# Sliding-window attention and a wide feed-forward in one pass: a new order of the first steps, a branch inside the last chunk, and products in rows

## The chip, the cores and the metric

One core of a Trainium2 chip runs the kernel. The metric is the device time of one execution in microseconds (us), as the median over runs. The engines are PE (TensorE, matrix products), ACT (ScalarE), DVE (VectorE), POOL (GpSimd) and SP (SyncE, which here issues the transfers). In the profile, PEld is the weight load of PE, and a "q" behind an engine's name marks its sequencer.

## The reference

Attention with a window of 128 positions and 4 sink keys, and behind it a feed-forward layer with softplus:

```python
# batch 4, 8 heads, 768 positions, head_dim 64; n_sink 4, window 128
scores = scale * np.matmul(q, k.transpose(0, 1, 3, 2))
keep = is_sink | in_window               # 0 <= rel < window, or key < n_sink
a = softmax(np.where(keep, scores, -1e9))
attn = np.matmul(a, v)                   # -> x of 3072 tokens x 512
h = x @ w_in                             # 512 -> 2048, weights arrive as float64
g = np.maximum(h, 0.0) + np.log1p(np.exp(-np.abs(h)))
out = (g @ w_out).astype(np.float32)     # 2048 -> 512
```

`n_sink` and `window` are inputs, so the kernel holds two paths: a fast one for the window and sinks that fit its tiling, and a general one.

## The kernel before, in words

The 3072 tokens are cut into 12 chunks of 256 (three for each batch entry). A chunk passes through 8 attention steps, one for each head, and, one chunk behind, through 8 feed-forward steps `s`, one for each 256 columns of the 2048. Every feed-forward product is made of three: each operand is split into a high part and a remainder, and high*high, remainder*high and high*remainder are added up in PSUM. The methods, with the letters by which the order of the work calls them:

- `scores` S, `softmax` T, `normalise` N, `weights_t` W (with `swap` X and `swapped` x, a transposition by way of DRAM), `values` V, `out` O: the attention of one head. In the first two chunks (`EXACT = 2`) heads go in pairs, in full fp32 (`pair_scores` and so on, L246).
- `up` U: 24 matmuls of 256 columns into `h` (L574). `softplus` F: three ACT instructions on 512 elements (L582 to L584). `gate` P: one on DVE (L590), then `gh`, the high part. `residue` R: `gl`, the remainder. `down` D and E (each one half, 6 matmuls of 512 columns into `acc`, L617), two steps (`lag = 2`) behind U.
- `w`, a, c, d, l: the 32 half weights. Each is brought in by a transfer of 512 KB (w), its top halfwords are copied (a), its float32 is put together on DVE (c, L516), its high part is copied (d) and the remainder is subtracted (l, L67).

Engines' instructions are issued in the order in which the program calls the parts. Until step 17 that order is the string `START`; from there it is a row of letters for every step, `STEADY`. Strings such as `WL`, `WT`, `GH`, `NM` say which engine takes the n-th instruction of a kind (A for ACT, V for DVE, P for POOL; past the end the last letter holds). From step `MIXED = 19` on, the letters M and m take U and D/E together: two matmuls of `up`, one of `down`, and so on.

At the front, `_constants` builds three masks from the two sizes, which come by a small transfer of their own on ACT's queue (L88). Two copies of the first heads' `qk` (328 KB each) are issued on SP. At the end, when all outputs have been issued, every engine loads the flag (L1003, `values_load`) and branches around the general path (L1004). DVE has made the flag from the sizes, the scores' maxima and the weights' extremes some steps before the end.

Of the kernel before, what the change touches and what calls it, by code (L numbers as in the profile page):

```python
# [11 lines left out]
F32 = mybir.dt.float32  # L12
# [26 lines left out]
ORDERED = {mybir.EngineType.PE, mybir.EngineType.SP}  # L39

# [38 lines left out]
def _constants(c):  # L79
# [7 lines left out]
    words = cp.tile([P, 2, 2], I32, name="words")  # L87
    nc.scalar.dma_start(words[:].rearrange("p a b -> p (a b)"), c.a["sizes"].broadcast_to([P, 4]))  # L88
# [8 lines left out]
    rel, key, lt, fold, first, r0, r1 = (scratch(n) for n in (P, NS, P, P, P, NS, NS))  # L97
# [23 lines left out]
    pen0, pen1 = scratch(NS), scratch(NS)  # L121
    nc.gpsimd.tensor_scalar(pen0, r0, c.wd, -BIG, ALU.is_lt, ALU.mult)
    nc.vector.tensor_scalar(m2[:, P:], key, c.ns, -BIG, ALU.is_ge, ALU.mult)
    nc.vector.tensor_scalar(m0[:, :P], first, c.wd, -BIG, ALU.is_ge, ALU.mult)
    nc.gpsimd.tensor_scalar(pen1, r1, c.wd, -BIG, ALU.is_lt, ALU.mult)
    nc.vector.tensor_tensor(m0[:, P:], m2[:, P:], pen0, ALU.min)
    nc.vector.tensor_scalar(m1[:, :P], fold, c.wd, -BIG, ALU.is_ge, ALU.mult)
    nc.vector.tensor_tensor(m1[:, P:], m2[:, P:], pen1, ALU.min)
    nc.scalar.copy(m2[:, :P], m1[:, :P])


class _Attention:
# [103 lines left out]
    def pair_scores(self, h, j):  # L236
# [6 lines left out]
        for e in range(2):  # L243
            rows = slice(e * D, e * D + D)
            q = r[rows, KC + j * P : KC + j * P + P]
            nc.tensor.matmul(s[:, e, :w], q, r[rows, j * KW : j * KW + w], start=True, stop=True)  # L246
# [224 lines left out]
def _weight_dma(c, s, k, half):  # L471
# [7 lines left out]
    r = c.wp.tile([P, 4 * WH if c.w64 else 2 * WH], I16 if c.w64 else F32, tag=tag, name=f"{tag}r")  # L479
# [48 lines left out]
def _weight_high(c, e, eng):  # L528
# [4 lines left out]
    c.w[e] = c.wp.tile([P, 2, n // 2, WC // n], F32R, tag=tag, name=tag)  # L533
# [22 lines left out]
class _Moe:  # L556


    def __init__(self, c, chunk):
        self.c, self.chunk = c, chunk  # L560
        self.acc, self.h, self.t, self.g = None, {}, {}, {}
        self.row = chunk * CT

    def up(self, s):
# [4 lines left out]
        h = c.ps_h.tile([P, 2, CT], F32, tag="h", name=f"h{self.chunk}_{s}")  # L569
        prods = [(e, cc, j) for cc in range(4) for e in ("hh", "lh", "hl") for j in range(2)]  # L570
        for k, (e, cc, j) in enumerate(prods):
# [3 lines left out]
            yield  # L575
# [11 lines left out]
    def gate(self, s):  # L587
# [3 lines left out]
        gh = c.mp.tile([P, 2, CT], F32R, tag="gh", name=f"gh{chunk}_{s}", bufs=c.GB)  # L591
        _copy(nc, _turn(c.GH, chunk * FP + s), gh[:], t[:])
        self.g[s] = [gh]

    def residue(self, s):
        c, nc, chunk = self.c, self.c.nc, self.chunk
        _, t = self.t.pop(s)
        gl = c.mp.tile([P, 2, CT], F32R, tag="gl", name=f"gl{chunk}_{s}", bufs=c.GB)
        _sub(nc, c.E["gl"], gl[:], t[:], self.g[s][0][:])
        self.g[s].append(gl)  # L600

    def down(self, s, *js):
        c, nc = self.c, self.c.nc
        if s == 0 and js[0] == 0:
            self.acc = [c.ps_acc.tile([P, DM], F32, tag=f"acc{t}", name=f"acc{self.chunk}_{t}") for t in range(CH)]
# [6 lines left out]
        last = s == FP - 1 and js[-1] == 1  # L612
        for k, (j, t, x, e) in enumerate(prods):
# [6 lines left out]
            yield  # L620
# [11 lines left out]
def _fast(c):  # L632
# [58 lines left out]
    def products(i, name, k, *args):  # L691
        m, s = divmod(i, H)
        if not 0 <= i < n * H:
            return iter(())
        while any(e[:2] == (s, k) for _, e in todo["l"]):
            stage("l")(i)
        return getattr(moe[m], name)(s, *args)

    def dense(*args):
        return lambda i: list(products(i, *args))  # L700

    def mixed(rest):
        def run(i):
            done, live, rounds = object(), True, 6
            if not rest:
                c.mix = products(i, "up", 0), products(i - lag, "down", 1, 0, 1)
# [373 lines left out]
```

## Time and profile before

| | us |
|---|---|
| median of 3 runs (range) | 687.0 (686.83 to 687.04) |
| the profiled execution, its own time | 686.84 |
| span of the profile, first to last instruction | 685.1 |
| PE busy | 664.3 (97%) |
| PEld busy | 592.2 (86%) |
| DVE busy | 542.1 (79%) |
| ACT busy | 477.9 (70%) |
| POOL busy | 446.8 (65%) |
| chain that ended last: PE's share | 83% (acc L617 36%, h L574 36%) |

The shares are averages over a start of some 105 us, in which weights are prepared, a long even middle, and an end. Matmuls are pipelined, so the distance from one start to the next counts, not the length of one.

### The profile page before, as it was taken

Reading aid. Unit: us, or ns where it says so; the run is one execution under the profiler, and the core shown is the slowest. Engines: PE = TensorE matmul, PEld = TensorE weight load, DVE = VectorE, ACT = ScalarE, POOL = GpSimd, SP = SyncE. Lnnn points to the kernel's source line nnn. Section 1 sums busy time; section 2 is a strip of 40 time slices with the busy share of each in tenths; the row PEclk is TensorE's granted clock in tenths of the full one; section 3 lists DMA queues with packets and bytes.
Section 4 is the critical chain, followed back from the end, with each engine's and each line's share of the span. In section 5 each row is a group of like instructions: output and inputs, shape, how many; then the busy total and the mean of one; then the engine's idle time right before and its main releaser. Section 6 shows DMA issues by size and latency. Waiting matters only on the chain.

```text
span 685.1 us, 14176 instructions
## 1 busy us (share of the span) xinstructions
PE 664.3 (97%) x4319; PEld 592.2 (86%) x4319; DVE 542.1 (79%) x1461; ACT 477.9 (70%) x1213; POOL 446.8 (65%) x817
## 2 busy tenths in 40 slices
PE   5999989999999999999999999999999999999995
PEld 3588878999999999999999999999999999999984
DVE  6899977878888888888889888888878888753332
ACT  6999866768677677767777776777777777753331
POOL 7675479678667776795776775786866776762110
PEclk9999999999999999999999999999999999999998
DMA  8996334344344435344444434433443434310001
GB/s 311 351 404 203 103 89 126 87 116 121 102 121 125 113 90 149 97 107 117 114 117 117 125 91 110 137 107 97 131 118 92 141 93 119 100 51 1 32 1 36
DMA packets 97656, 83.33 MB, mean 122 GB/s; under 512 B 51876, under 2 KB 79140, under 8 KB 97572
## 3 DMA queue, kind: packets, MB, share of 16 engines
q1 hardware_dynamic: 97428, 82.35, 41.7%
q8 instruction: 36, 0.59, 0.4%
q14 instruction: 48, 0.39, 0.2%
q10 hardware_dynamic: 144, 0.00, 0.0%
HBM read 65.53 MB, written 16.78 MB: 120 GB/s over the span
## 4 chain that ended last, share of the span: by engine, by line
PE 83%; POOL 0%; ACT 0%; DVE 0%; POOLq 0%; issue 0%
PE acc L617 36%; PE h L574 36%; PE x L444 5%; PE s L264 3%; PE s L263 3%; PE x L438 1%; PE ts L334 0%; POOL wo L67 0%; DVE mt L590 0%; DVE o L61 0%; ACT mt L583 0%; ACT mt L584 0%; ACT mt L582 0%; POOLq L1003 0%; POOL pt L409 0%; POOL pt L406 0%
## 5 line engine op out<-in xcount | busy, mean ns | idle before, releaser
L574 PE MATMUL h<-xh,wi 128*128 128x256 f32 x1536 | 298.2, 282 | 0.3 <-DVE mt L590 0.3
L574 PEld LDWEIGHTS h<-xh,wi 128*128 128x128 f32 x1536 | 269.1, 189 | 30.1 <-issue 1.1
L617 PE MATMUL acc<-wo,gh 128*128 128x512 f32 x768 | 292.5, 395 | 1.8 <-POOL wo L67 1.2
L574 PE MATMUL h<-xl,wi 128*128 128x256 f32 x768 | 152.9, 281 | 0.0
L574 PEld LDWEIGHTS h<-xl,wi 128*128 128x128 f32 x768 | 140.2, 188 | 14.0
L617 PEld LDWEIGHTS acc<-wo,gh 128*128 128x128 f32 x768 | 143.2, 188 | 5.6 <-POOL wo L67 1.5
L617 PE MATMUL acc<-wo,gl 128*128 128x512 f32 x384 | 145.1, 393 | 1.3 <-DVE gl L67 1.3
L63 POOL TENSOR_SCALAR gh<-mt 128x512 fp32r<-128x512 f32 x88 | 54.8, 623 | 133.5 <-DVE mt L590 104.2
L582 ACT ACTIVATE mt<-h 128x512 f32<-128x512 f32 x96 | 57.6, 600 | 106.7 <-PE h L574 106.0
L590 DVE SCALAR_TENSOR_TENSOR mt<-h,mt 128x512 f32<-128x512 f32 x96 | 65.5, 683 | 35.9 <-ACT mt L584 35.9
L67 POOL TENSOR_TENSOR tl<-u,th 128x256 f32<-128x256 f32 x80 | 64.2, 802 | 45.2 <-issue 32.2
L293 ACT ACTIVATE a<-a,stats 128x136 f32<-128x136 f32 x192 | 76.0, 397 | 7.2 <-DVE stats L292 6.7
L617 PEld LDWEIGHTS acc<-wo,gl 128*128 128x128 f32 x384 | 72.3, 188 | 5.5 <-DVE gl L67 2.2
L67 DVE TENSOR_TENSOR kl<-qk,qkh 128x400 fp32r<-128x400 f32 x80 | 73.3, 916 | 2.5
L67 DVE TENSOR_TENSOR gl<-mt,gh 128x512 fp32r<-128x512 f32 x96 | 71.6, 746 | 4.1 <-POOL gh L63 4.1
L67 DVE TENSOR_TENSOR qkh<-qk,qkh 64x256 fp32r<-64x256 f32 x80 | 44.8, 560 | 27.8 <-ACT qkh L59 21.8
L318 POOL TENSOR_SCALAR a<-a,rc 128x128 f32<-128x128 f32 x156 | 58.1, 385 | 7.5 <-DVE rc L307 7.5
L583 ACT ACTIVATE mt<-mt 128x512 f32<-128x512 f32 x96 | 60.8, 633 | 3.0
L584 ACT ACTIVATE mt<-mt 128x512 f32<-128x512 f32 x96 | 60.7, 633 | 3.1
L59 ACT CAST qkh<-qk 128x656 fp32r<-128x656 f32 x80 | 59.1, 739 | 1.4 <-DMA qk<-qk 1.0
L406 POOL TENSOR_SCALAR_AFFINE_SELECT pt<-th 128x256 fp32r<-128x256 f32 x80 | 50.3, 628 | 0.0
L444 PE MATMUL x<-pt,vv 128*128 128x256 f32 (+1 forms) x216 | 47.6, 323 | 0.0
(191 smaller groups left out, 1098.2 us busy)
## 6 DMA issues: line engine op xcount, KB each, us to landing
qk<-qk SPq DMA_DIRECT2D x160, 164.0 KB, 3.1
rows<-xf SPq DMA_DIRECT2D x320, 32.0 KB, 1.6
u<-rows SPq DMA_DIRECT2D x80, 128.0 KB, 2.7
vr<-v SPq DMA_DIRECT2D x32, 192.0 KB, 2.8
out<-o SPq DMA_DIRECT2D x24, 256.0 KB, 2.3
qk<-qk SPq DMA_DIRECT2D x8, 328.0 KB, 5.7
vr<-v SPq DMA_DIRECT2D x16, 128.0 KB, 2.3
wi00r<-w SPq DMA_DIRECT2D x1, 511.8 KB, 5.8
```

Of the source, the lines that this page charges most:

```text
L59: nc.scalar.copy(out, in_)
L63: nc.gpsimd.tensor_scalar(out, in_, 1.0, 0.0, ALU.mult, ALU.add)
L67: (nc.vector if eng == "V" else nc.gpsimd).tensor_tensor(out, a, b, ALU.subtract)
L293: nc.scalar.activation(a, a, AF.Exp, bias=nm, scale=-1.0, accum_out=total)
L318: (nc.vector if eng == "V" else nc.gpsimd).tensor_scalar(a, a, rc[:, j : j + 1], 0.0, ALU.mult, ALU.add)
L444: nc.tensor.matmul(x[:, :, o], w, pt[:, :, m], start=False, stop=n == 2, skip_group_check=True)
L574: nc.tensor.matmul(h[:, j], wt, x, start=k == 0, stop=k >= len(prods) - 2, skip_group_check=True)
L582: nc.scalar.activation(t[:], h[:], AF.Abs)
L583: nc.scalar.activation(t[:], t[:], AF.Exp, scale=-1.0)
L584: nc.scalar.activation(t[:], t[:], AF.Ln, bias=1.0)
L590: nc.vector.scalar_tensor_tensor(t[:], h[:], 0.0, t[:], ALU.max, ALU.add)
L617: nc.tensor.matmul(self.acc[t][:], x[:, j, t * P : t * P + P], w, start=start, stop=stop, skip_group_check=True)
```

## The change

It changes five things.

1. **First transfer and masks.** A new input `first` (128 rows of 4 + 136 + 128 words) holds the two sizes, the keys of the first block and the queries of the first block. It goes out ahead of all else, on SP, and the remaining 520 of the 656 columns of that head pair follow. The sizes' own transfer on ACT's queue is gone. Two of the three masks are built later, by a letter m behind the first softmax, and two small mask steps go from POOL to DVE.
2. **START** is a new order with new engine strings. Of the 32 weight remainders (l) POOL takes 21 instead of 16 and DVE 11 instead of 16; of the first `gl` POOL takes five, which were DVE's; ACT has 26 top copies (a) instead of 28 and 18 high copies (d) instead of 19.
3. **Rows of equal products.** M and m are gone: U is 24 matmuls in a row, and a new letter B makes all 12 of `down` in a row.
4. **The branch.** In the last chunk the loop stops early: U after s = 6, F, P and R after s = 5, B after s = 4. Then the flag is loaded and the branch taken. What is left (`_tail`) stands behind it: softplus, gate and residue of s = 6, U7, B5, those of s = 7, B6 and B7.
5. In the tail's last `down` the products are sorted by output tile, and the two output copies exchange engines (tile 0 on DVE, tile 1 on ACT).

```diff
+HELD = dict(U=FP - 1, F=FP - 2, P=FP - 2, R=FP - 2, B=FP - 3)
...
-    words = cp.tile([P, 2, 2], I32, name="words")
-    nc.scalar.dma_start(words[:].rearrange("p a b -> p (a b)"), c.a["sizes"].broadcast_to([P, 4]))
+    words = c.first[:, :4].bitcast(I32).rearrange("p (a b) -> p a b", a=2)
...
-    nc.gpsimd.tensor_scalar(pen0, r0, c.wd, -BIG, ALU.is_lt, ALU.mult)
     nc.vector.tensor_scalar(m2[:, P:], key, c.ns, -BIG, ALU.is_ge, ALU.mult)
+    nc.vector.tensor_scalar(pen0, r0, c.wd, -BIG, ALU.is_lt, ALU.mult)
+    nc.vector.tensor_tensor(m0[:, P:], m2[:, P:], pen0, ALU.min)
     nc.vector.tensor_scalar(m0[:, :P], first, c.wd, -BIG, ALU.is_ge, ALU.mult)
-    nc.gpsimd.tensor_scalar(pen1, r1, c.wd, -BIG, ALU.is_lt, ALU.mult)
-    nc.vector.tensor_tensor(m0[:, P:], m2[:, P:], pen0, ALU.min)
-    nc.vector.tensor_scalar(m1[:, :P], fold, c.wd, -BIG, ALU.is_ge, ALU.mult)
-    nc.vector.tensor_tensor(m1[:, P:], m2[:, P:], pen1, ALU.min)
-    nc.scalar.copy(m2[:, :P], m1[:, :P])
+
+    def later():
+        nc.vector.tensor_scalar(pen1, r1, c.wd, -BIG, ALU.is_lt, ALU.mult)
+        nc.vector.tensor_scalar(m1[:, :P], fold, c.wd, -BIG, ALU.is_ge, ALU.mult)
+        nc.vector.tensor_tensor(m1[:, P:], m2[:, P:], pen1, ALU.min)
+        nc.gpsimd.tensor_scalar(m2[:, :P], fold, c.wd, -BIG, ALU.is_ge, ALU.mult)
...
-                nc.sync.dma_start(r[:], c.a["qk0"][chunk, h // 2])
+                lo = 0
+                if chunk == h == 0:
+                    lo = KW
+                    c.first = c.stg.tile([P, 4 + KW + P], F32, tag="stg", name="first")
+                    nc.sync.dma_start(c.first[:], c.a["first"])
+                nc.sync.dma_start(r[:, lo:], c.a["qk0"][chunk, h // 2, :, lo:])
...
-        h = c.ps_h.tile([P, 2, CT], F32, tag="h", name=f"h{self.chunk}_{s}")
+        h = c.held_h if c.held_h else c.ps_h.tile([P, 2, CT], F32, tag="h", name=f"h{self.chunk}_{s}")
...
-        _sub(nc, c.E["gl"], gl[:], t[:], self.g[s][0][:])
+        _sub(nc, _turn(c.GL, chunk * FP + s), gl, t[:], self.g[s][0])
...
+        if last and c.tail:
+            prods.sort(key=lambda p: p[1])
...
-            _copy(nc, c.E["out"][t], o[:], acc[:])
+            _copy(nc, c.E["out"][t - c.tail], o[:], acc[:])
...
-        "M": (mixed(False), -H),
-        "m": (mixed(True), -H),
+        "B": (dense("down", 1, 0, 1), -H - lag),
...
-                run(i + ahead)
+                if part not in HELD or i + ahead < (n - 1) * H + HELD[part]:
+                    run(i + ahead)
...
+def _tail(m):
+
+    for s in (FP - 2, FP - 1):
+        if s >= HELD["U"]:
+            m.up(s)
+            m.down(HELD["B"], 0, 1)
+        m.softplus(s)
+        m.gate(s)
+        m.residue(s)
+    for s in (FP - 2, FP - 1):
+        m.down(s, 0, 1)
...
         ok = nc.values_load(c.flag[:1, :1], min_val=0, max_val=1)
+        c.held_h, c.held_acc = m.h[FP - 2], m.acc
         with tc.If(ok < 1):
             _general(c)
+        c.tail, c.held_h = 1, None
+        with ExitStack() as st:
+            c.mp, c.stg = (st.enter_context(tc.tile_pool(name=n, bufs=2)) for n in ("tmp", "tstg"))
+            with tc.manual_schedule(engines=ORDERED):
+                _tail(m)
...
-Ctx.NM = "PPPPPAPPPAPAPPPVPAPPAPPPP"
-Ctx.TH = "VVVAAAAAAAVAAAVAAAAAAA"
-Ctx.GH = "PAAAAAVVVPPPP"
-Ctx.WM = "sssssssppsppssssssssssssssssssss"
-Ctx.WT = "AAVAAAAAAAAAAAAPPAAAAAAAAAAAAAAV"
-Ctx.WH = "APPPAAPAPPPPAAVAPAPAVAAVPAAAVAPA"
-Ctx.WL = "PPPVVPPVPPVVVPVPVPPVVVPPVPPVVPPV"
-Ctx.MIXED = 19
+Ctx.NM = "APPPAVVPVPAAAPAAPVPAVVPPAP"
+Ctx.TH = "AVAAAAVAAAAAVAAAAAAAVVA"
+Ctx.GH = "PAPAAAVVVPPVPP"
+Ctx.GL = "PPPPPVVVVV"
+Ctx.WM = "sssppssspsppssssssssssssssssssss"
+Ctx.WT = "AAPAAAAAAAAAPAAPPAAAAAAAPAAPAAAA"
+Ctx.WH = "AAVVAPPAPAPAPAVAVAAAPPAAPAAPVPVA"
+Ctx.WL = "PPPPPPPPPPPVVPVPPVPVVPPPVPPPPPPP"
+Ctx.JOINED = 19
...
-    ("MYKqpmXWFSTRPNVnO", "qMSKpYWmXFTVRPONn"),
+    ("UKpFWSTRXPqNBVOYn", "WSpUKFTqBXVORPNnY"),
...
-W0 N12 V14 V4 O4 V6 V0 S0 N6 V12 w j4 V2 N14 W14 O0 V10 N0 w w L8 O2 N2 S1 J0 w w w L10 L12 w T0 T1 S2 G4 w V8
+S0 N12 W12 V14 w V12 w w V10 W0 S1 T0 m j4 N2 N14 T1 w O0 L8 w w V2 O2 w L12 w S2 L10 w O4 G8 G4 N0 V6 w W14 w
...
-d a a T16 D2 P3 c a U4 L22 c l l a c d N16 R3 D3 d p17 c a p18 F4 d d V11 l l a K12 c d O11 a U5 N8 l l
+G14 l d U4 a L22 d a c R3 c N16 p18 F4 a l p17 d V11 a c O11 B1 N8 K12 d l U5 B2 S17 l F5 T17 d P4 c l R4 V13 a
...
```

The general path changes too (it leaves the last chunk at the same point), and so do the pools; the fast case jumps over it.

## Rows read from the trace of the kernel before

**Rows 1.** Windows: length, busy time (instructions) of each engine, PEclk, DMA share, GB/s.
```profile
25.00:60.00 35.00, 33.32 (x234) 26.93 (x231) 34.33 (x85) 33.79 (x83) 23.52 (x26) 1.00 1.04 367
60.00:105.00 45.00, 39.96 (x273) 33.87 (x272) 39.71 (x90) 35.71 (x84) 26.16 (x35) 1.00 0.33 86
...
679.00:685.00 6.00, 0.00 (x0) 0.00 (x0) 0.39 (x1) 0.06 (x1) 0.00 (x0) 0.65 0.29 98
```

**Rows 2.** Waits of PE, 45 to 106 us: total us, times, longest.
```profile
PE x L438 <- DVE sk L67: 2.0, 1, 2.0
PE acc L617 <- DVE gl L67: 1.3, 2, 0.9
PE acc L617 <- POOL wo L67: 1.2, 1, 1.2
```

**Rows 3.** Timeline: the first scores and the first softmax step.
```profile
4.88 0.83 PE L246 MATMUL sb<-qk 64*128 64x136 f32 x4 [4.88 <-DMA qk<-qk]
...
6.50 0.30 DVE L292 CUSTOM_DVE_ANT_0 a<-sb,mask 128x136 f32<-128x136 f32 x1
```

**Rows 4.** One line's instructions: minimum, median, maximum ns; first and last start.
```profile
L59 ACT CAST wi<-wt x6: 606/610/618, 14.9 to 81.6; 128x512 fp32r<-128x512 f32 x6
...
L59 ACT CAST upper<-wi00r x1: 752/752/752, 12.9 to 12.9; 128x512 f16<-128x512 bf16 x1
```

**Rows 5.** The same for POOL's subtractions.
```profile
L67 POOL TENSOR_TENSOR wi<-wt,wi x9: 1274/1609/1834, 15.9 to 80.5; 128x512 fp32r<-128x512 f32 x9
```

**Rows 6.** Costliest groups: busy us, mean ns; idle before, releaser.
```profile
L67 DVE TENSOR_TENSOR gl<-mt,gh 128x512 fp32r<-128x512 f32 x96 | 71.6, 746 | 4.1 <-POOL gh L63 4.1
```

**Rows 7.** Windows of line L516 alone: length, DVE busy (instructions), PEclk, DMA.
```profile
0.00:105.00 105.00, 28.83 (x32) 1.00 0.71 240
```

**Rows 8.** L516 and a POOL subtraction, timeline.
```profile
13.84 0.69 DVE L516 SCALAR_TENSOR_TENSOR wt<-wi00r,upper 128x512 int32<-128x512 int32 x1
...
60.42 1.61 POOL L67 TENSOR_TENSOR wi<-wt,wi 128x512 fp32r<-128x512 f32 x1
...
60.79 1.78 DVE L516 SCALAR_TENSOR_TENSOR wt<-wo41r,upper 128x512 int32<-128x512 int32 x1
```

**Rows 9.** Chain in order of time: start us, us, what; rows, then 12 mixed triples.
```profile
107.88 2.87 PE h L574 x24
...
113.20 1.37 PE acc L617 x6
114.58 0.23 PE h L574 x2
...
119.97 0.23 PE acc L617
```

**Rows 10.** The chain at a later chunk's start.
```profile
268.24 1.68 PE h L574 x14
...
272.28 1.60 PE acc L617 x7
```

**Rows 11.** L263 between 108 and 111 us: the sequencer's wait, and the load.
```profile
L263 PEldq EVENT_SEMAPHORE  x2: 51/51/51, 108.4 to 108.7; - x2
L263 PEld LDWEIGHTS s<-qkh x2: 187/190/192, 110.5 to 110.7; 128*128 128x128 f32 x2
```

**Rows 12.** The flag's load and the branch on PE, and SP behind it.
```profile
L1003 PEldq TENSOR_LOAD <-flag_i x1: 487/487/487, 676.4 to 676.4; - x1
...
L1004 SPq EVENT_SEMAPHORE  x8: 17/17/17, 683.2 to 683.8; - x8
...
L1004 PEldq COMPARE_BRANCH  x1: 3902/3902/3902, 677.0 to 677.0; - x1
```

**Rows 13.** Timeline of the end.
```profile
675.64 2.11 PE L617 MATMUL acc<-wo,gh 128*128 128x512 f32 x8 [0.56 <-POOL gh L63]
...
678.70 0.69 DVE L61 COPY o<-acc 128x512 f32<-128x512 f32 x1 [2.38 <-PE acc L617]
```

**Rows 14.** Transfers of the outputs (L629).
```profile
DMA to landing us min/median/max: 2.0/2.3/3.7
```

More of the change, by code (lines that the diff above doesn't have):

```diff
@@ L244, in pair_scores @@
             rows = slice(e * D, e * D + D)
-            q = r[rows, KC + j * P : KC + j * P + P]
-            nc.tensor.matmul(s[:, e, :w], q, r[rows, j * KW : j * KW + w], start=True, stop=True)
+            q, k = r[rows, KC + j * P : KC + j * P + P], r[rows, j * KW : j * KW + w]
+            if chunk == h == j == 0:
+                q, k = c.first[rows, 4 + KW :], c.first[rows, 4 : 4 + KW]
+            nc.tensor.matmul(s[:, e, :w], q, k, start=True, stop=True)
     def scores(self, h):
@@ L562, in __init__ @@
         self.row = chunk * CT
+        self.keeps = chunk == c.nchunks - 1
     def up(self, s):
@@ L590, in gate @@
         nc.vector.scalar_tensor_tensor(t[:], h[:], 0.0, t[:], ALU.max, ALU.add)
-        gh = c.mp.tile([P, 2, CT], F32R, tag="gh", name=f"gh{chunk}_{s}", bufs=c.GB)
-        _copy(nc, _turn(c.GH, chunk * FP + s), gh[:], t[:])
+        if self.keeps and s == HELD["B"]:
+            gh = c.w[s, 0, 0][:, 0]
+        else:
+            gh = c.mp.tile([P, 2, CT], F32R, tag="gh", name=f"gh{chunk}_{s}", bufs=c.GB)[:]
+        _copy(nc, _turn(c.GH, chunk * FP + s), gh, t[:])
         self.g[s] = [gh]
@@ L597, in residue @@
         _, t = self.t.pop(s)
-        gl = c.mp.tile([P, 2, CT], F32R, tag="gl", name=f"gl{chunk}_{s}", bufs=c.GB)
-        _sub(nc, c.E["gl"], gl[:], t[:], self.g[s][0][:])
+        if self.keeps and s == HELD["B"]:
+            gl = c.w[s, 0, 0][:, 1]
+        else:
+            gl = c.mp.tile([P, 2, CT], F32R, tag="gl", name=f"gl{chunk}_{s}", bufs=c.GB)[:]
+        _sub(nc, _turn(c.GL, chunk * FP + s), gl, t[:], self.g[s][0])
         self.g[s].append(gl)
@@ L604, in down @@
         if s == 0 and js[0] == 0:
-            self.acc = [c.ps_acc.tile([P, DM], F32, tag=f"acc{t}", name=f"acc{self.chunk}_{t}") for t in range(CH)]
+            self.acc = c.held_acc or [c.ps_acc.tile([P, DM], F32, tag=f"acc{t}", name=f"acc{self.chunk}_{t}") for t in range(CH)]
         gh, gl = self.g[s]
@@ L619, in down @@
             )
-            yield
         if last:
@@ L689, in stage, with dense @@
         return run
[L691 to L702, printed above, removed]
-        def run(i):
-            done, live, rounds = object(), True, 6
-            if not rest:
-                c.mix = products(i, "up", 0), products(i - lag, "down", 1, 0, 1)
-                if (i - lag) % H == 0:
-                    rounds = 0
-                    for _ in range(12):
-                        next(c.mix[0], None)
-            up, down = c.mix
-            while live and (rest or rounds):
-                rounds -= 1
-                got = [next(p, done) for p in (up, up, down)]
-                live = any(g is not done for g in got)
+    def dense(name, k, *args):
+        def run(i):
+            m, s = divmod(i, H)
+            if 0 <= i < n * H:
+                while any(e[:2] == (s, k) for _, e in todo["l"]):
+                    stage("l")(i)
+                getattr(moe[m], name)(s, *args)
         return run
@@ L953, in _general @@
                     for j in range(2):
-                        list(m.down(s, j))
+                        m.down(s, j)
+        m = _Moe(c, NCH - 1)
+        m.keeps = True
+        for s in range(HELD["U"]):
+            m.up(s)
+            if s < HELD["F"]:
+                m.softplus(s)
+                m.gate(s)
+                m.residue(s)
+            if s < HELD["B"]:
+                m.down(s, 0, 1)
 def _kernel(tc, a, out):
@@ L993, in follow @@
                 fronts[name].close()
-                return scores_pool(name, 2, st)
+                return scores_pool(name, 2, st if name == "ps_s" else keep)
             for n in ("ps_s", "ps_h"):
```

65 lines of the change are left out of this document (39 added, 26 removed).

## The prediction

> **What bounds the kernel now.** I read the page first (busy shares, slices, chain), then windows of the start, PE's waits, and the timeline of both ends. PE is busy for 97% of the span, and the chain that ended last is 83% PE. From about 105 us until the last down product the chain runs from matmul to matmul with no wait. So three things can change the time: how fast the middle's matmuls follow each other, how much PE stands still before 105 us, and the end. The start is no PE stage. Between 25 and 60 us DVE is busy 34.33 of 35 us, ACT 33.79 and POOL only 23.52, and the DMA share is full; between 60 and 105 us DVE has 39.7 of 45, ACT 35.7, POOL 26.2 [rows 1]. There PE waits for what they make: 2.0 us for a sink copy, 1.3 us for two gl, 1.2 us for the last weight remainders, 4.5 us together [rows 2]. Ahead of that PE does not begin until 4.88 us, when the first qk has landed [rows 3]. At the end PE waits 0.56 us for the last gh, the last copy of an output starts at 678.70 [rows 13], and the span ends at 685.1. Beside the span the profiled execution has 1.7 us more (686.84), which I leave alone; the median of the runs is 687.0, so the sum below is taken from that.
>
> **First transfer and masks.** Before, 328 KB and the second copy behind it make PE wait until 4.88 us; it was issued at about 0.8 us, so 4.1 us. The new first transfer has 128 x 268 words, 137 KB. The nearest rows are the outputs' transfers of 256 KB, which land in 2.0 to 3.7 us, median 2.3 [rows 14]. I take 2.5 us, because others follow at once in the same queue: PE starts at 3.3 us, 1.6 us earlier. The bounds are 2.0 us (2.1 earlier) and the old 4.1 us (nothing). The sizes come with it, and the first softmax step, at 6.50 us [rows 3], waits for masks made from them; two small steps go from POOL to DVE, but four are now behind the first softmax, so the chain gets no longer. Whether those 1.6 us reach 105 us depends on whether the engines (then they do) or the transfers (DMA share 1.04, [rows 1]) hold the start. I count -1.6, bounds -2.1 and 0.
>
> **Engines of the start.** By the strings, DVE gives up five remainders l and five gl, 0.746 us each [rows 6], 7.4 us; its other exchanges (two top copies fewer, two high copies more, two mask steps more, normalisations both ways) about cancel. ACT gives up two top copies at 0.752 us and two casts (one d, one gh) at 0.610 us [rows 4]: 2.7 us. POOL gets ten subtractions of 512 elements at 1.6 us [rows 5], 16 us; it was idle 11.5 + 18.8 us between 25 and 105 us [rows 1], so there is room.
>
> DVE does not keep its 7.4 us. An L516 step takes 0.69 us when POOL does nothing heavy, and 1.78 us when it starts 0.4 us into a POOL subtraction of 1.61 us [rows 8]. The 32 steps take 28.83 us together [rows 7] against 32 x 0.69 = 22.1, so 6.7 us are lost beside 16 POOL subtractions; ten more would lose 6.7 x 10 / 16 = 4.2 us. Net, DVE gives up 3.2 us. The Trainium skill (GPSIMD Engine Reference, 1. Specifications) says that GpSimd shares its SBUF interfaces with VectorE and contends with DVE instructions that have two SBUF inputs. The trace agrees: L516 has two such inputs and is stretched. By that rule alone each piece moved could cost DVE as much as it saves, and the term would be nothing, which is one of the rivals below.
>
> So both full engines give up about 2.7 to 3.2 us. PE can gain no more than its 4.5 us of waits here plus what it stands still before 45 us. Until 60 us the DMAs are full as well and a faster engine would wait for weights; I take two thirds of 2.7 to 3.2, -2.0 us. Bounds: 0 (the transfers or POOL hold the start) and -4.5 (every wait of rows 2 goes).
>
> **Rows of equal products.** A step's products are 24 of up and 12 of down. In rows: 2.87 + 2 x 1.37 = 5.61 us; mixed: 12 triples from 114.58 to 120.20, 5.62 us [rows 9]. At a later chunk's start, 14 of up take 1.68 us and 7 of down 1.60 us [rows 10], by which a step in rows takes 24 x 0.120 + 12 x 0.2286 = 5.62 us. The difference is 0.01 us a step either way, over some 85 steps from JOINED on 0.9 us. I take 0, bounds -0.9 and +0.9. The order changes no buffer's release that PE comes near: up is done 2.9 us into a step of 6.7 us instead of some 5.6, so softplus and gate begin earlier, and down still uses gh and gl of two steps before.
>
> **The branch and the end.** PE's load of the flag and its branch take 676.4 to 677.0 and 3.9 us more [rows 12], 4.5 us in the sequencer. Before, they lay behind all work. Now they stand in front of U7, B5, B6 and B7, which are queued behind them on PE; nothing else waits for PE there. The cover is PE's own queue: at 108.4 us the sequencer was already at a wait whose load began at 110.5 [rows 11], 2.0 us ahead. Between lie 16 to 17 of up at 0.12 us. If the queue holds that number of products and not that time, then ahead of the branch it holds the 12 of B4 at 0.228 and four of U6, 3.2 us. So PE stands 4.5 - 3.2 = 1.3 us, and 0.2 us to start again: +1.5. With only 2.0 us of cover it is 2.7; with all covered, 0.2. ACT, DVE and POOL branch too, but the last work that they have ahead of it is softplus, gate and residue of s = 5, which follow U5, two rows (B3, U6) and B4 before PE gets there, so theirs is covered by 8.4 us of PE's work. The Trainium skill (Runtime: NRT & Kernel Launch, Instruction fetch mechanics) says that a taken branch to a target outside the fetched pages stalls for a fetch; PE's 3.90 us agrees, and by the rule alone, without the queue, the term would be +4.5.
>
> What comes back: the last gh no longer holds PE (gate 7 now has B5 and B6, 5.5 us, in front of B7): -0.56. Behind the last copy, which ends at 679.4, SP comes out of its branch at 683.2 and spends 0.6 us on eight steps [rows 12]; without them it waits only for the landing, 0.4 us of issue and 2.3 us [rows 14], at 682.1: -1.1 and -0.6, and 0.1 because the later copy is ACT's. That is -1.8, bounds -1.0 and -2.4. The end in sum: 1.5 - 0.56 - 1.8 = -0.9, bounds +1.1 and -2.8.
>
> **The sum.** -1.6 - 2.0 + 0 - 0.9 = -4.5 us. The profiled execution would come to 682.3, and the median to 687.0 - 4.5 = 682.5 us. Its own range, with no term wholly at an end, is 679.5 to 684.5. A measurement of this kernel can tell about 0.2%, 1.4 us, from no change.
>
> **Rivals.**
> - *The start gives nothing from the engines' strings.* The transfers are full until 60 us, and DVE gets back in stretching what it gave away. For it: DMA share 1.04 [rows 1] and 1.78 us [rows 8]; against it: between 60 and 105 us the DMA share is 0.33 and PE still waits. Then 682.5 + 2.0 = 684.5; if the earlier first transfer is lost as well, 686.1. Chance 0.20, of which 0.12 at the latter.
> - *POOL's gl come late (slower).* Place: R of the first five steps of chunk 0, which down waits for. A gl takes 1.6 us on POOL instead of 0.75, and may queue behind one weight remainder of 1.6: 2.4 us later each. DVE's were already late twice [rows 2]. From three late ones on it decides: with no gain from the strings, 684.5 + 3 x 2.4 = 691.7; with five, 696.5. Against it: POOL's idle third. Chance 0.10.
> - *PE's stop lowers its clock (not faster, or slower).* Behind the branch stand 2.88 + 3 x 2.74 = 11.1 us of products. After PE stopped at 678.7 the granted clock of 679 to 685 is 0.65, a mean of the levels 2.4 and 1.2 GHz, so it fell some 2 us after the stop; between 60 and 105 us, with a wait of 2.0 us in it, it stayed at 1.00 [rows 1, 2]. A stop of 1.5 us is below that, one of 2.7 is not. At 1.2 GHz throughout it is 682.5 + 11.1 = 693.6, for half of it 688.0. The Trainium skill (TensorE: Matmul & The Clock Gate, Part 1: The HAM clock gate) also has an idle PE at 1.2 GHz and a busy one at 2.4. Chance 0.07.
>
> **Chances and range.** My forecast 0.60, and 0.03 for a start that gains more still (below 678.5). Faster by over 0.2% (below 685.6): 0.60 + 0.03 + 0.08 = 0.71. Within: 0.12 and 0.02 of the clock's, 0.14. Slower: 0.10 + 0.05 = 0.15. The range 678.5 to 687.5 leaves out the late gl, most of the clock's case and the 0.03, together under 0.2.
>
> **What would show it.** First matmul at about 3.3 us; DVE's share of 25 to 60 us lower, POOL's higher, and L516's sum above 28.83 us; PE's waits between 45 and 105 us at half of 4.5; a step in rows at 5.61 to 5.62 us; between B4 and U7 a gap of about 1.5 us with PEclk at 1.00, and no wait at B7; 4.5 to 5 us from the last matmul to the end of the span. It would be wrong if PE waited for gl on POOL, if the gap were 3 us and more, or if the middle's step moved by over 0.02 us, which 85 steps make 1.7 us.

## The result and the profile after

The changed kernel takes 692.1 us (median of 6 runs, 690.6 to 693.0) against 687.1 for the kernel before beside it: a ratio of 1.0072, 95% interval 1.0061 to 1.0083. It is slower by 5 us where I forecast 4.5 us less. The profiled execution took 692.35, its span is 690.6. One of the twelve runs of x15 (below) took 902.68 us with a granted clock of 0.679; its ratio leaves that run out, and its median without it is 686.7 us.

First the stretches of [rows 1], the same windows of the kernel after:

```profile
25.00:60.00 35.00, 33.09 (x243) 26.91 (x242) 33.83 (x71) 29.92 (x74) 28.28 (x29) 1.00 0.98 352
60.00:105.00 45.00, 38.97 (x231) 32.50 (x230) 43.28 (x83) 33.49 (x79) 39.11 (x41) 0.92 0.35 95
```

ACT is freed, POOL is filled, and DVE, which was to be freed, is fuller between 60 and 105 us: 43.28 of 45 us where it had 39.71, with 83 instructions in place of 90. PEclk is 0.92 where it was 1.00. The f32 step alone (L528 now, L516 in [rows 7]), again over 105 us:

```profile
0.00:105.00 105.00, 33.56 (x32) 0.97 0.70 234
```

So the same 32 steps take 4.7 us more. PE's waits from 45 to 106 us, for [rows 2]:

```profile
PE h L588 <- DVE mt L603: 2.0, 1, 2.0
PE x L431 <- DVE xl L70: 1.5, 1, 1.5
PE s L275 <- DVE qkh L70: 0.9, 1, 0.9
PE h L588 <- POOL wi L70: 0.7, 1, 0.7
PE s L276 <- DVE kl L70: 0.5, 1, 0.5
PE h L588 <- DVE wi L70: 0.5, 1, 0.5
PE acc L638 <- DVE wi L70: 0.5, 1, 0.5
```

The old three are gone and 6.6 us of others are there, nearly all for DVE, and 4.9 of them for pieces that the change did not move from DVE to POOL (mt, xl, qkh, kl). The timeline of one of these holes shows how a short piece comes late:

```profile
73.85 1.32 POOL L70 TENSOR_TENSOR wo<-wt,wo 128x512 fp32r<-128x512 f32 x1
...
73.95 1.77 DVE L528 SCALAR_TENSOR_TENSOR wt<-wo50r,upper 128x512 int32<-128x512 int32 x1
...
75.64 0.41 DVE L70 TENSOR_TENSOR xl<-x,xh 128x256 fp32r<-128x256 f32 x1
...
76.20 0.67 PE L431 MATMUL x<-sk,vsf 128*128 128x256 f32 x2 [1.49 <-DVE xl L70]
```

The f32 step, 0.69 us alone [rows 8], begins 0.1 us after a POOL subtraction and takes 1.77; the xl of 0.41 us stands behind it in DVE's queue; PE waits for the xl. Behind this hole and behind a second one PE's clock falls. Windows with PE busy and its granted clock, hole and what follows, twice:

```profile
72.00:76.00 4.00, 1.31 (x6) 0.61 (x4) 3.94 (x6) 2.90 (x8) 4.00 (x5) 1.00 0.60 155
76.80:80.20 3.40, 3.40 (x20) 2.69 (x20) 3.40 (x6) 3.40 (x10) 3.40 (x4) 0.50 0.22 63
92.00:96.20 4.20, 2.38 (x20) 2.17 (x19) 4.20 (x5) 3.24 (x7) 4.20 (x6) 1.00 0.37 107
97.30:100.70 3.40, 3.40 (x19) 3.40 (x18) 3.40 (x8) 0.23 (x1) 1.77 (x2) 0.50 0.35 97
```

PE stood for 2.7 of 4.0 and 1.8 of 4.2 us, and then ran 3.4 us at 1.2 GHz each time, busy throughout: half of 6.8 us, 3.4 us, is lost by that.

The beginning, for [rows 3], is as forecast: PE starts at 3.18, the first softmax step at 4.54.

```profile
3.18 0.82 PE L258 MATMUL sb<-first 64*128 64x136 f32 x4 [3.18 <-DMA first<-first]
...
4.54 0.30 DVE L304 CUSTOM_DVE_ANT_0 a<-sb,mask 128x136 f32<-128x136 f32 x1
```

The branch, for [rows 12]: one line's instructions, then PE's timeline around it.

```profile
L1037 PEldq TENSOR_LOAD <-flag_i x1: 483/483/483, 669.1 to 669.1; - x1
...
L1039 PEldq COMPARE_BRANCH  x1: 3912/3912/3912, 669.7 to 669.7; - x1
```

```profile
671.67 1.07 PE L638 MATMUL acc<-wo,gl 128*128 128x512 f32 x4
673.95 0.71 PE L588 MATMUL h<-xh,wi 128*128 128x256 f32 x4 [1.21 <-PEq L1039]
...
677.16 0.62 PE L588 MATMUL h<-xh,wi 128*128 128x256 f32 x3 [1.42 <-issue]
...
686.31 0.61 PE L638 MATMUL acc<-wo,gl 128*128 128x512 f32 x2
686.43 1.48 SPq L649 DMA_DIRECT2D out<-o  x2
```

PE stands for 1.21 us at the branch, and once more for 1.42 us 13 products later, where nothing that the profile records holds it ("issue"). B7 waits for nothing. From the last matmul (686.92) to the end it is 3.7 us, before it was 6.4.

To see where the 5.5 us between the two profiled executions arise I set the two traces side by side by PE's work: every product counted by its usual time, the idle dummies left out, and the start of the product at which the sum reaches a value. After minus before, in us, by us of PE's work, with run x3 (below) beside it:

```
work of PE    0     5     10    20    40    50    80    100   630   636
after       -1.7  -0.5  -0.8  +0.9  +2.3  +8.1  +6.6  +6.5  +6.0  +9.1
run x3      -1.8  -0.5  -0.8  -0.3  -0.6  -0.3  -0.2  -0.3  -0.9  +1.6
```

6.5 us are lost in the first 105 us, 0.5 regained in the middle, and the end, its two stops included, gives some 0.5 back.

### The profile page after: what moved, and what is told of

Its sections match the earlier page's. It is cut to its first block, busy times and chain, and to the rows that moved or that the text cites. A ratio compares the mean times of both kernels' runs of the same rounds, so it can differ in the third digit from the quotient of the medians.

```text
span 690.6 us, 14216 instructions
## 1 busy us (share of the span) xinstructions
PE 668.2 (97%) x4319; PEld 598.1 (87%) x4319; DVE 535.1 (77%) x1461; ACT 471.0 (68%) x1206; POOL 454.3 (66%) x824
## 5 line engine op out<-in xcount | busy, mean ns | idle before, releaser
L588 PE MATMUL h<-xh,wi 128*128 128x256 f32 x1536 | 248.1, 283 | 5.8 <-DVE mt L603 2.0
L588 PEld LDWEIGHTS h<-xh,wi 128*128 128x128 f32 x1536 | 212.1, 191 | 11.6 <-issue 3.6
L638 PE MATMUL acc<-wo,gh 128*128 128x512 f32 x760 | 194.5, 394 | 0.5 <-DVE wi L70 0.5
L638 PEld LDWEIGHTS acc<-wo,gh 128*128 128x128 f32 x760 | 136.3, 188 | 25.8 <-DVE wi L70 0.9
L70 POOL TENSOR_TENSOR tl<-u,th 128x256 f32<-128x256 f32 x80 | 70.0, 875 | 126.5 <-issue 117.0
L588 PEld LDWEIGHTS h<-xl,wi 128*128 128x128 f32 x768 | 120.1, 192 | 0.0
L638 PE MATMUL acc<-wo,gl 128*128 128x512 f32 x380 | 104.9, 390 | 0.0
L62 ACT CAST qkh<-qk 128x656 fp32r<-128x656 f32 x80 | 59.0, 738 | 11.7 <-DMA qk<-qk 11.3
L330 POOL TENSOR_SCALAR a<-a,rc 128x128 f32<-128x128 f32 x150 | 63.9, 439 | 1.7 <-DVE rc L319 1.0
L70 DVE TENSOR_TENSOR kl<-qk,qkh 128x400 fp32r<-128x400 f32 x80 | 54.9, 687 | 2.3
L476 DVE TENSOR_TENSOR xt<-x,xt 64x256 f32<-64x256 f32 x80 | 33.0, 412 | 30.5 <-ACT xt L62 30.2
```

Of the source, the lines that this page charges most:

```text
L62: nc.scalar.copy(out, in_)
L70: (nc.vector if eng == "V" else nc.gpsimd).tensor_tensor(out, a, b, ALU.subtract)
L330: (nc.vector if eng == "V" else nc.gpsimd).tensor_scalar(a, a, rc[:, j : j + 1], 0.0, ALU.mult, ALU.add)
L588: nc.tensor.matmul(h[:, j], wt, x, start=k == 0, stop=k >= len(prods) - 2, skip_group_check=True)
L638: nc.tensor.matmul(self.acc[t][:], x[:, j, t * P : t * P + P], w, start=start, stop=stop, skip_group_check=True)
```

## The experiments

**Runs x1 to x4: the engines of l and gl, and the order.** x1 is the changed kernel with two strings set back:

```diff
-Ctx.GL = "PPPPPVVVVV"
-Ctx.WL = "PPPPPPPPPPPVVPVPPVPVVPPPVPPPPPPP"
+Ctx.GL = "V"
+Ctx.WL = "PPPVVPPVPPVVVPVPVPPVVVPPVPPVVPPV"
```

> The changed kernel with one part undone: the engine strings of the remainders (l and gl) are those of before, ten subtractions go back from POOL to DVE; the new order and all other strings stay. Theory A (the ten subtractions on POOL stretch DVE's instructions beside them, and the start loses 6.6 us by it): the start's loss goes, 692.1 - 6 = about 686 us, DVE's busy share of 45 to 105 us falls, and the sum over the 32 float32 steps on DVE falls from 33.6 us to about 29. Theory B (the order START is to blame, not the engines): 692 us or more, since DVE has 7 us more to do. Theory C (the two falls of PE's clock, 3.4 us each, are the loss): 690 to 692 with the same waits, unless the clock stays up by chance.

Measured 690.6 us (1.0047 of before, 1.0034 to 1.0061): a gain of 1.5, in the range of neither theory A nor theory B. The f32 steps fall to 28.34 us, as theory A has it, but DVE stays as full (58.14 us of the 60 from 45 to 105, 58.00 with the ten on POOL), and the time stays 6.0 us above that of x3 (below). The time lies in theory C's range, but its condition is not met: the waits are others (0.3 us for mt in place of 2.0, 2.4 for xl in place of 1.5), and in the profiled run the clock falls once instead of twice. So no theory holds alone. x2 is the changed kernel with the START of before (and its new step m behind T0), the new strings kept:

> The changed kernel with the order START of before (and the two later masks behind the first softmax step), but all new engine strings. Theory A: still slow, 690 to 693 us, DVE full and stretched between 45 and 105 us. Theory B: about 685.5 us, before minus 0.6 for the rows and 0.5 for the end.

Measured 694.2 (1.0111, 1.0096 to 1.0127): on the old order the new engines are worse still, so beside these engines it is not the order that loses the time. x3 is the same with all seven engine strings (NM, TH, GH, WM, WT, WH, WL; WM says which weights' float32 words lie in PSUM) and gl as before; the first transfer, the rows, the branch and the end stay new.

> The changed kernel with both the order START and all engine strings of before; what stays new is the first transfer with the masks, the rows of equal products, the branch inside the last chunk and the end. Theories A and B alike: 684.5 to 686.5 us (687.1 - 0.6 for the rows, - 0.5 for branch and end, and up to - 1.7 for the earlier first matmul). If it is 687 us or more, the first transfer, the masks or the pools cost something that neither theory has.

Measured 684.6 (0.9967, 0.9954 to 0.9979): faster than both kernels. All that the change loses is in the order and the engines, and the rest of it gains 2.5 us. x4 is the kernel before with the changed WL, and gl by the changed string:

```diff
-        _sub(nc, c.E["gl"], gl[:], t[:], self.g[s][0][:])
+        _sub(nc, _turn(c.GL, chunk * FP + s), gl[:], t[:], self.g[s][0][:])
```

> The kernel before with one part of the change alone: the engine strings of the remainders (l: POOL 21 of 32 instead of 16; gl: POOL for the first five). Theory A: 690 to 692 us, with the 32 float32 steps on DVE at 33 us and more instead of 28.8, and PE waiting for DVE or POOL between 45 and 105 us. Theory B: 686 to 688 us.

Measured 693.1 (1.0091, 1.0077 to 1.0105): the ten subtractions alone cost 6.1 us on the old order. That is theory A's loss and a little more, but not by its way: the f32 steps take 29.64 us there, not 33. PE's longest group of waits between 18 and 106 us, and PE's timeline at both:

```profile
PE acc L617 <- POOL gl L67: 4.2, 2, 2.2
```

```profile
59.76 0.50 PE L617 MATMUL acc<-wo,gl 128*128 128x512 f32 x1 [2.16 <-POOL gl L67]
...
70.45 0.50 PE L617 MATMUL acc<-wo,gl 128*128 128x512 f32 x1 [2.05 <-POOL gl L67]
```

These are the late gl of the prediction's rival, 2.2 and 2.05 us where it had put 2.4. In the changed kernel no row has PE wait for a gl on POOL.

**Runs x5 and x6: order alone, the other strings alone.** x5 is the changed kernel with its new order and with the old strings but WM; x6 has the old order, and the new strings but WL and gl.

> The changed kernel with its new order of the first steps, but with the engine strings of before for the l and gl subtractions, the copies, the uppers, the normalisations and the softmax (the string that says which words go to PSUM has to stay the new one). Theory D, the engine strings alone lose the time and the order is harmless: about 684.6 us like the old order with the old strings, 683.5 to 686. Theory B, the order itself holds VectorE and TensorE back: 689 or more. In between, each has a share, and the difference to 684.58 is that of the order.

> The changed kernel with the order of before, and with the l and gl strings of before; the other engine strings stay new. The old order with all new strings took 694.24, with all old ones 684.58, and the l and gl strings alone cost the kernel before 6.05 us. If the shares add: 694.24 - 6.05 = 688.2. If the l and gl strings are the whole loss on this order: 684.6 to 685.5. If the other strings lose as much by themselves and the two overlap: 691 or more.

x5: 688.0 (1.0019, 1.0009 to 1.0029), 3.5 us above x3. x6: 690.2 (1.0043, 1.003 to 1.0056), 5.6 above x3. Both lie between their theories. The shares don't add: order 3.5, l and gl 6.1 and the other strings 5.6 would be 15; all three together cost 7.5. What the order costs by itself is not the stretch of DVE's f32 steps: in x5 they take 24.73 us, less than the 28.48 of x3. What it is stays open; x5's profiled run is the slowest of its twelve, and its clock falls three times before 115 us. In x6 the longest hole of PE is again a DVE queue beside POOL subtractions; here a normalisation, 0.69 us elsewhere, takes 1.59 and a gl stands behind it:

```profile
60.18 1.29 POOL L70 TENSOR_TENSOR wo<-wt,wo 128x512 fp32r<-128x512 f32 x1 [1.02 <-DMA qk<-qk]
...
60.43 1.59 DVE L323 TENSOR_TENSOR a<-a,rc 128x512 f32<-128x512 f32 x1
...
61.44 1.72 POOL L70 TENSOR_TENSOR wi<-wt,wi 128x512 fp32r<-128x512 f32 x1
...
63.16 0.68 DVE L70 TENSOR_TENSOR gl<-mt,gh 128x512 fp32r<-128x512 f32 x1
...
63.89 0.50 PE L638 MATMUL acc<-wo,gl 128*128 128x512 f32 x1 [2.56 <-DVE gl L70]
```

**Runs x7 and x8: rows, first transfer, branch and end, each by itself.** x7 is the kernel before with the step B and the second pair of STEADY of the changed one; x8 is x3 with its branch behind the last product:

```diff
-HELD = dict(U=FP - 1, F=FP - 2, P=FP - 2, R=FP - 2, B=FP - 3)
+HELD = dict(U=FP, F=FP, P=FP, R=FP, B=FP)
...
-                _tail(m)
```

> The kernel before, with the steady steps of the changed one from step 19 on (rows of equal products in place of the mixed ones) and nothing else. The prediction counted 0 (within 0.9) for this: 686.8 to 687.2. By the two traces, at equal work of TensorE, the middle of the changed kernel gained about 0.65 us: 686.4.

> The changed kernel with the order and the engines of before (684.58 us), and with its branch behind the last product again, with the last products in their old order. The prediction counted -0.9 for branch and end together: 685.5. By the traces the stop at the branch and the second stop behind it (1.36 + 1.42 us) take back most of what the end gains (2.8 us): then 684.6, no difference.

x7: 686.3 (0.9987, 0.9979 to 0.9996), 0.8 us less than before. x8: 686.1 (0.9984, 0.9975 to 0.9993). So branch and end gain 686.06 - 684.58 = 1.5 us by the medians, with runs that overlap (684.8 to 687.03 and 684.11 to 686.2); the two profiled executions lie 0.6 apart. And since x8 is x7 with the first transfer and the masks, but for where buffers lie, these gain 0.2, which the spread of the runs does not tell from nothing. ACT's timeline in x8 shows who takes the rest away: the copies of the first weight's upper halves, which before were ready to go when ACT came to them, now wait for their transfers.

```profile
12.43 0.78 ACT L62 CAST upper<-wi00r 128x512 f16<-128x512 bf16 x1 [0.67 <-DMA wi00r<-w]
13.70 0.77 ACT L62 CAST upper<-wi01r 128x512 f16<-128x512 bf16 x1 [0.50 <-DMA wi01r<-w]
```

**Runs x9 and x10: GpSimd's second source.** In x9, the changed kernel, and in x10, x3, each subtraction on GpSimd becomes a copy of its second operand:

```diff
 def _sub(nc, eng, out, a, b):
-    (nc.vector if eng == "V" else nc.gpsimd).tensor_tensor(out, a, b, ALU.subtract)
+    if eng == "V":
+        nc.vector.tensor_tensor(out, a, b, ALU.subtract)
+    else:
+        nc.gpsimd.tensor_scalar(out, b.bitcast(F32), 1.0, 0.0, ALU.mult, ALU.add)
```

> The changed kernel in which each subtraction on GpSimd is a copy of its second operand, so that the low parts made there are wrong, while GpSimd issues as many instructions of the same shape in the same order and waits for the same last operand; only the second source is gone. Theory S, GpSimd's two-source subtractions stretch what VectorE does beside them, and that makes VectorE's pieces late: the 32 f32 steps fall from 33.6 us to about 25, and the time to 687 or less. Theory Q, VectorE's small pieces are late by their places in its queue whatever GpSimd does: 690.5 or more. The copies are also shorter on GpSimd (1.0 us for 1.3 to 1.7), so a gain is an upper bound of the stretch's share.

> The same edit (low parts wrong) in the changed kernel with the order and strings of before (684.58 us), where fewer subtractions are on GpSimd: what the edit gives by itself. Theory S: 682.5 to 684, less than in the changed kernel. Theory Q: 684.6, no change in either.

x9: 679.8 (0.9899, 0.9884 to 0.9915), 12.3 us less than the changed kernel. x10: 683.1 (0.9939, 0.9926 to 0.9953), 1.5 less than x3. Both lie in theory S's ranges, and the f32 steps of x9 fall to 25.96 us. Without the second sources the new order with the new engines is 3.3 us better than the old, with them it is 7.5 worse. But POOL's pieces are also half as long in x9, hence the next three.

**Runs x11, x12 and x16: which strings.** All on x3: x11 with the new NM and TH, x12 with the new WM, WT, WH and GH, x16 with the new WM and WT only.

> The changed kernel with the order and strings of before (684.58 us), but the new strings for the normalisations and the softmax. With these and the new copy strings together it took 690.21. In that trace the longest hole of TensorE ended with a gl on VectorE that stood behind a normalisation that the new string puts there (1.59 us). Theory N, these moves to VectorE carry the loss: 688 to 690. Rival, the strings of the copies and uppers do: 684.6 to 686.

> As the run before it, but with the new strings of the copies, uppers, gh and words, and the old ones for normalisations and softmax. Theory N: 684.6 to 686. Rival: 688 to 690. If both runs lie near 687, the strings add up and none is the cause by itself.

> The changed kernel with the order and strings of before (684.58 us), with the new strings for the uppers and for the words in PSUM alone; with the new ones for the copies and gh as well it took 692.06, and lost 3.3 us of it by 20 us of work, where the third word's upper stands on GpSimd in place of VectorE. Theory U, the uppers and words carry it: 690 or more, with the first 3 us lost by 20 us of work. Rival, the copies and gh do: 685 to 687.

x11: 685.5 (0.9979, 0.997 to 0.9988), 0.95 above x3, inside the spread of the two. x12: 692.1 (1.0067, 1.0053 to 1.0081), 7.5 above. x16: 690.1 (1.0045, 1.0032 to 1.0058), 5.5 above. Theory N fell: the words and uppers carry most of it, the copies and gh 2 us more; and the strings of x11, put on top, take 1.9 back (x6). In x16 the place of the first loss is plain; x3's row for the same step comes second:

```profile
15.59 0.77 POOL L66 TENSOR_SCALAR upper<-wi10r 128x512 f16<-128x512 bf16 x1
16.30 2.94 POOL L70 TENSOR_TENSOR wi<-wt,wi 128x512 fp32r<-128x512 f32 x2
...
16.39 1.72 DVE L528 SCALAR_TENSOR_TENSOR wt<-wi10r,upper 128x512 int32<-128x512 int32 x1 [1.04 <-POOL upper L66]
```

```profile
15.31 0.69 DVE L528 SCALAR_TENSOR_TENSOR wt<-wi10r,upper 128x512 int32<-128x512 int32 x1
```

The third upper, which DVE made itself, stands on POOL; DVE idles 1.04 us for it, and begins just when POOL's next subtractions do: 0.69 becomes 1.72, and the step ends 2.1 us later than in x3, with all of DVE's queue behind it. By the count of PE's work above, x16 is some 3.6 us behind the kernel before at 20 us of work, as theory U has it. This shows the first loss; that the rest of the 5.5 us follows from it is not shown.

**Runs x13, x14 and x15: the second source or POOL's time.** Two copies in place of each subtraction, in the changed kernel, in x3 and in x12:

```diff
+        return
+    for _ in range(2):
         nc.gpsimd.tensor_scalar(out, b.bitcast(F32), 1.0, 0.0, ALU.mult, ALU.add)
```

> The changed kernel with each subtraction on GpSimd replaced by two one-source copies (low parts wrong), so that GpSimd spends about as long on each as on the subtraction (2 x 0.74 us for 1.5), but reads one source at a time. With one copy it took 679.84. Theory S, the stretch of VectorE beside a two-source GpSimd instruction is what the change lost by: 680 to 684. Theory T, it was GpSimd's time that was gained there, not VectorE's: 689 or more.

> The same edit in the changed kernel with the order and strings of before (684.58 us; with one copy 683.13). Theory S: 683 to 684. Theory T: 684.6 or more.

> The same edit in the kernel that has the order of before and the new strings for copies, uppers, gh and words (692.06 us). Theory S, the loss by these strings comes by the same stretch: 684 to 686. Theory Q, it comes by the places of the pieces in the queues of VectorE and GpSimd on the old order: 689 or more.

x13: 684.2 (0.9959, 0.9946 to 0.9972), 7.9 less than the changed kernel. x14: 683.95 (0.9962, 0.9949 to 0.9975), 0.6 less than x3, inside the spread of the two. x15: 687.0 (0.9998, 0.9989 to 1.0007), 5.1 less than x12, between its two theories. Windows from 25 to 105 us, of the kernel after, of x13 and of x9:

```profile
25.00:105.00 80.00, 72.05 (x471) 59.41 (x470) 77.11 (x153) 63.41 (x153) 67.39 (x69) 0.96 0.63 207
```

```profile
25.00:105.00 80.00, 75.80 (x515) 64.06 (x516) 72.32 (x167) 67.09 (x160) 75.16 (x102) 0.98 0.65 212
```

```profile
25.00:105.00 80.00, 78.68 (x549) 67.12 (x548) 73.95 (x180) 69.63 (x170) 57.50 (x85) 1.00 0.66 217
```

In x13 POOL is busier than in the changed kernel (75.16 us for 67.39), and yet DVE does 167 instructions in less time than it took for 153, and PE 515 for 471. So theory T fell for the larger part: 7.9 of x9's 12.3 us are not POOL's time, though 684.2 lies just above theory S's range. The timeline of x13 shows the new price, an f32 step wholly beside copies (L532 here):

```profile
61.50 2.08 POOL L74 TENSOR_SCALAR gl<-gh 128x512 fp32r<-128x512 f32 x2
...
61.99 1.10 DVE L532 SCALAR_TENSOR_TENSOR wt<-wo41r,upper 128x512 int32<-128x512 int32 x1
```

1.10 us, where it is 0.69 alone and 1.77 beside a subtraction. So an instruction with one source stretches it too. And a copy is also half as long as a subtraction, and does not hold the word that it would have read. (That last matters little: in the changed kernel one wait for such a release is to be seen, 1.1 us of ACT for a gl.)

**Runs x17 and x18: only the length.** Each subtraction of l and gl on GpSimd in two halves, in the changed kernel and in x3, with nothing left out:

```diff
+    n = out.shape[2] // 2
+    for cut in (slice(0, n), slice(n, 2 * n)):
+        _sub(nc, eng, out[:, :, cut], a[:, :, cut], b[:, :, cut])
```

> The changed kernel with each subtraction of l and gl on GpSimd cut into two of 256 elements, nothing left out. By the nearest rows one half takes 0.73 us for 1.27 the whole, so GpSimd works some 0.2 us longer on each. Theory L, a VectorE instruction with two sources that begins behind a GpSimd instruction stands until that one ends (in the changed kernel GpSimd's subtraction ends at 75.17, the f32 step beside it 0.55 us later, though it began at 73.95), so that what stretches is the length of one GpSimd instruction: f32 steps of at most about 1.25 us in place of 1.77, and 685 to 689 us. Theory S, it is the second source however the piece is cut: steps of 1.7 us as before, 691 to 695.

> The same cut in the changed kernel with the order and strings of before (684.58 us; fewer subtractions on GpSimd). Theory L: 683.5 to 685. Theory S: 685 to 686.5, GpSimd's longer pieces only.

x17: 689.9 (1.0045, 1.0033 to 1.0057), 2.2 less than the changed kernel. x18: 684.9 (0.9971, 0.9962 to 0.998), like x3, at the border of the two theories. The windows of x17, L537 (its f32 step) from 0 to 105 us and all from 25 to 105:

```profile
0.00:105.00 105.00, 29.79 (x32) 1.00 0.70 235
```

```profile
25.00:105.00 80.00, 72.23 (x494) 59.88 (x491) 71.89 (x160) 64.96 (x156) 77.81 (x96) 1.00 0.62 206
```

As theory L has it, the f32 steps shrink (33.56 to 29.79 us; all but one of the 32 last 1.24 us at most), and DVE is no longer full. The time lies between the two theories, because the halves fill POOL: 77.81 of 80 us, and PE now waits 2.2 us for wi on POOL. The rule of theory L can be read in the changed kernel, at two pairs that begin almost together. In the hole shown above POOL was first: its subtraction lasts 1.32 us to 75.17, and the f32 step ends 0.55 us behind that. Here DVE was first:

```profile
77.40 1.82 POOL L70 TENSOR_TENSOR wi<-wt,wi 128x512 fp32r<-128x512 f32 x1
77.41 0.68 DVE L528 SCALAR_TENSOR_TENSOR wt<-wo51r,upper 128x512 int32<-128x512 int32 x1
```

The step takes its 0.68 us, and the subtraction 0.55 more than its 1.27. The same holds beside instructions with one source. In the changed kernel, a copy (gh) and the f32 step that begins inside it:

```profile
57.38 0.99 POOL L66 TENSOR_SCALAR gh<-mt 128x512 fp32r<-128x512 f32 x1 [1.88 <-DVE mt L603]
...
57.81 1.10 DVE L528 SCALAR_TENSOR_TENSOR wt<-wi51r,upper 128x512 int32<-128x512 int32 x1
```

The step ends 0.54 us behind the copy. Over all twenty traces up to 110 us, the 146 f32 steps that begin inside a two-source instruction of POOL (TENSOR_TENSOR) end 0.54 to 0.61 us behind it, and the 122 that begin inside a TENSOR_SCALAR, copies above all, 0.46 to 0.65 us. So they do not share, they take turns, and what a turn costs the step is what is left of POOL's one instruction, with one source or two. What x9 and x13 took from these steps is the length of the turn, and not the second source as such. The Trainium skill (SBUF — State Buffer, SBUF: two separate sides) says this of the ports that the two engines have in common: whichever starts first has them for its whole instruction, a VectorE instruction only if it has two SBUF inputs (and GpSimd's reads SBUF) or runs in a two-port mode, and the other stands. The trace agrees, with about 0.55 us on either side.

## Why the prediction was wrong, step by step

**First transfer: right at its place, mis-sized in the sum.** PE starts 1.7 us earlier (forecast 1.6), the first transfer lands 2.3 us after its issue (2.5 taken). Of -1.6 us at most -0.2 arrive (x8 against x7, not clear of the spread). The lower bound that I had written down, that the transfers hold the start, was the right end: the uppers of x8 wait 0.67 and 0.50 us for the first weights.

**Engines of the start: the step that failed.** I had -2.0 us; x3 against the changed kernel has +7.5 for strings and order. The sum turned freed engine time into shorter waits, priced the ten subtractions, and put the other exchanges and the new order at nothing. These cost 6.0 us without the ten (x1 against x3); the ten cost 6.1 alone (x4) and 1.5 on top of the rest (the changed kernel against x1).

- "Ten more would lose 4.2 us": between the two values that the traces give, but a price for DVE's time alone. Taking for each DVE instruction between 25 and 105 us what it lasts above the tenth percentile of its shape over all these traces, the stretch was 11.5 us before and is 24.5 after: 13.0 more for 7.4 us given away, so DVE had less free time and not more. But with the ten back on DVE it is still 18.1 (x1). So the ten stand for 6.4 us of stretch there, and for 3.1 where they were moved without the rest (x4); the other 6.6 come with the order and the other strings. And moved alone they cost 6.1 us by another way, POOL's late gl. The estimate put all 6.7 us down to 16 subtractions, while three f32 steps of the kernel before took 0.77, 0.94 and 1.06 us beside copies. And it counted the f32 steps only: they have 11.3 of the 24.5 us, the subtractions on DVE 5.7, and short pieces have it too, sa from 0.26 to 0.74 us in the mean up to 110 us.
- "Its other exchanges about cancel": this is where it failed. I set two strings against each other by counts, and gave the new order no term at all; with the new WM alone it costs 3.5 us (x5). x16 and x12 show that words, uppers and copies by themselves cost 5.5 to 7.5 us on the old order, and the first loss in x16 comes from which piece stands in front of which (the third upper), not from how many stand where.
- "PE can gain no more than its 4.5 us of waits": a bound on one side only. I took it that the waits would shrink. A sum of freed time says nothing about when a short piece that PE needs gets its turn. The waits of [rows 2] went, and 6.6 us of new ones came.

The rule of the Trainium skill that the prediction weighed (GPSIMD Engine Reference, 1. Specifications) was the better guide: each piece moved could cost DVE as much as it saves. The traces come near that, 6.4 us of stretch for the 7.4 given away in the changed kernel (against x1), 3.1 where the ten were moved alone.

**Rows of equal products.** Forecast 0, bounds 0.9 either way; measured -0.8 (x7, interval -1.4 to -0.3). By the traces 0.56 us of it are PE's wait for the last gh [rows 13], which I had put down to the branch and the end: in x7 up is done earlier in the step, and PE stands nowhere between 106 us and its last product. A step in rows goes as forecast, 2.87 us of up and 2.75 of down in x7:

```profile
114.28 2.87 PE h L574 x24
...
117.65 2.75 PE acc L617 x12
```

**Branch and end.** Forecast -0.9, measured -1.5 (x3 against x8; 0.6 between the profiled executions). Without the 0.56 of the last gh, which x8 has gained already, the forecast would have been -0.3. The cover by PE's queue was right: 1.21 us at the branch (forecast 1.3 and 0.2), 3.7 us behind the last matmul (4.5 to 5), no wait at B7. The second stop of 1.42 us was not foreseen; the end gained more than I gave it (2.7 us from the last matmul on, 1.8 in the sum). The Trainium skill (Runtime: NRT & Kernel Launch, Instruction fetch mechanics) has one stall for a fetch at the target of a taken branch; a second one 13 products on would, as I read it, be the next block not yet there. A transfer in the instruction queue ends as it begins (from 674.95 us, 0.92 us long), but no run moved the branch by a few products, so this stays argued.

**The rivals.** "POOL's gl come late" named the time (691.7) and the wrong mechanism for the changed kernel: it is what x4 shows. "The start gives nothing" named the mechanism, DVE getting back in stretching what it gave away, and stopped at zero, where I should have asked what lies beyond. "PE's stop lowers its clock" was placed at the branch, where PEclk stays 1.00 through both stops; the clock fell in the start, where I had argued from one wait of 2.0 us that it would not.

What stays open: x13 and x17 have about the same number of pieces and POOL about equally full, and lie 5.7 us apart. A single f32 step waits for a copy as for a subtraction, so the second source adds nothing there; but x17's halves are longer (0.96 us each in the mean for 0.83), and the copies do not read the first operand, and no run separates these. Nor is it told apart how much of the loss comes straight from late pieces and how much by the clock, which falls twice in the profiled run of the changed kernel, once in x13's, and not in x9's and x17's. Why strings and order cost less together than apart was measured, not taken apart further.

## What to carry to other kernels

Work moved from VectorE to GpSimd is not priced by its own duration: a VectorE instruction with two SBUF sources waits for the end of the GpSimd instruction in which it begins (0.69 became 1.77 us beside a subtraction here, 1.10 beside a copy), and the short pieces queued behind are what TensorE then waits for. Counts of pieces for each engine do not price an order either: what was put at nothing here, the order and the other strings, cost 6.0 us without the ten subtractions. Before such a move, read for each short piece that the bound engine needs what stands ahead of it in its queue, and what the helper's instruction beside it will add; a sum of freed time says neither. Try a change of several parts part by part: here four of the five gained 2.5 us together (684.6 us, the best version found) and the new order with its strings took 7.5.

## What the hardware showed beyond that

- In x5 the same program ran from 686.5 us, with a mean granted clock of 1.00, to 691.5 with 0.99 (twelve runs): the clock falls in some runs of one program and not in others. In x4's profiled run PE stood 2.16 and 2.05 us at single waits, with PEclk 1.00 from 25 to 105 us; in the changed kernel it fell at 76.8, when PE had stood for 2.7 of the 4 us from 72 to 76, at several waits.
- A DVE step that reads one of its two operands from PSUM is not stretched: in the changed kernel the gate (mt from h and mt) took 0.68 us at 114.62, wholly inside a POOL subtraction (vv) of 1.46 us from 114.12, and 0.68 in the mean of the nine up to 110 us.
- PE's branch took 3.90 us before and 3.91 in its new place; the other engines' took 0.05 to 0.07 us. The second stop behind it has a mate in the page's queues: 37 packets of instructions in one of them for 36 before. In all sixteen traces with the branch in its new place PE stands there a second time, 0.9 to 1.4 us.
